# Three PSUM banks for transposed units, one for the products, in a fused attention and two-MLP kernel

## The chip, the cores and the metric

The kernel runs on one core of one Trainium2 chip. The metric is the device time of one execution in microseconds (us); lower is better. TensorE multiplies matrices into PSUM, VectorE, ScalarE and GpSimd do the work on elements, and SyncE issues the transfers (DMA). Each engine runs its own instructions in their order, and waits on counters that the other engines raise.

## What is computed

```python
scores = scale * np.matmul(q, k.transpose(0, 1, 3, 2))      # 2 batches, 12 heads, 448 x 64
scores = np.where(mask, -1000000000.0, scores)              # causal
scores = scores - np.max(scores, axis=-1, keepdims=True)
attn = np.exp(scores)
attn = attn / (np.sum(attn, axis=-1, keepdims=True) + 1e-09)
x = np.matmul(attn, v)                                      # heads side by side: 896 x 768
gate = 1.0 / (1.0 + np.exp(-(x @ w_gate)))
x = gate * (x @ w_val) @ w_out                              # 896 x 1536, then 896 x 768
h = x @ w_in                                                # 896 x 1024
ln = layer_norm(h * softmax(h)) * g_ln
out = ln @ w_out2
```

All of it is fp32. A factor of a matrix product is split into a high part and the rest, its low part, and three products (high with high, high with low, low with high) are added up in PSUM.

## The kernel before

The attention comes first, for twelve pairs of heads (0 to 11). Its order is written out by hand: the table `STEPS` holds for each piece of work a step number, an engine and a function; pair p does the piece with number n at step 8p + n. At every step the loop goes through TensorE ('E'), ScalarE ('A'), VectorE ('D'), SyncE ('S') and GpSimd ('P'), and takes an engine's pieces in the order of the table. So eight steps make one period, in which three pairs are worked on: pair p begins with its scores, pair p - 1 is transposed and multiplied with v, and the product of pair p - 2 is scaled and put away. One period on the engines:

- TensorE. `sc_mm(p)` (L352, L365) writes the masks and the score products into PSUM tiles s. Then, for pair p - 1, `tr_mm` (L435) transposes the exponentials in four units t, numbered 0 to 3 (four 128 x 128 blocks each, one PSUM bank each), and `pv_mm` (L466) multiplies them with v in eight chunks, all into one bank x. A period holds: scores of p; chunk 3; unit 0; chunks 4, 5; unit 1; chunks 6, 7; unit 2; chunks 0, 1; unit 3; chunk 2. Chunks 3 to 7 end the product of p - 2, chunk 0 begins that of p - 1.
- VectorE. `sc_max` (L380) takes row maxima of the scores; `tr_lo` (L231) forms the low part of a transposed unit; `prep_q_lo` (L252) the low part of q; `recips` (L400, L401) the reciprocal row sums; `x_mul` (L472) scales the finished product x into xf.
- ScalarE. `sc_exp` (L392) does the exponentials, `tr_hi` (L442) copies the high part of a unit, `x_hi` (L223) that of the scaled product. In a period: unit 3; `x_hi`; exponential of score tile 3, first head; unit 0; three more exponentials (tile 3, second head; tile 0, both heads); unit 1; tile 2; unit 2; tile 1.
- GpSimd. High parts of q and k (`prep_q_hi` L236, `prep_k_hi` L225), low part of k (`prep_k_lo` L231), both parts of v, the sums and `x_lo`.
- SyncE. `rs_rows` (L406, tile rd) writes the reciprocals to DRAM and `rs_bcast` (L412, tile rb) reads them back, spread over 64 partitions, for `x_mul`; `load_qk` (L214) and `load_v` (L219) fetch later pairs, `dma_next` (L100) the raw MLP weights (768 KB a chunk).

The PSUM pools (L201 to L203) are two banks for units (`ps_t`), two for products (`ps_x`) and four for scores (`ps_s`). A new tile of a pool waits until all that reads the tile which held its bank is done: with two banks, unit 2 waits for the `tr_lo` of unit 0 two units earlier, and a product for the `x_mul` two pairs earlier.

After the attention come gate and value products (L639), the output product (L669), the second MLP's products (L701, L762), with weights that arrive chunk by chunk. The loop that the steps run in, and the pieces that the change touches, are printed here.

Of the kernel before, what the change touches and what calls it, by code (L numbers as in the profile page):

```python
# [43 lines left out]
def attn_moe_moe2(ctx: ExitStack, tc: tile.TileContext, qk, v, w_gv, w_out, w_in2, w_out2, g_ln, out):  # L44
# [149 lines left out]
    with ExitStack() as actx:  # L194
# [3 lines left out]
        ptp = actx.enter_context(tc.tile_pool(name="ptp", bufs=2, side="right"))  # L198
        xfp = actx.enter_context(tc.tile_pool(name="xfp", bufs=2, side="right"))
        drm = actx.enter_context(tc.tile_pool(name="drm", bufs=2, space=bass.MemoryType.DRAM))  # L200
        ps_t = actx.enter_context(tc.tile_pool(name="ps_t", bufs=2, space=PSUM, reuse_waits="tile"))  # L201
        ps_x = actx.enter_context(tc.tile_pool(name="ps_x", bufs=2, space=PSUM, reuse_waits="tile"))
        ps_s = actx.enter_context(tc.tile_pool(name="ps_s", bufs=2, space=PSUM, reuse_waits="tile"))  # L203

        NH = B * H
# [38 lines left out]

        def prep_k_lo(p):
            sub('P' if p else 'D', qk_sp[p][:, 3], qk_raw[p][:, 1], f32(qk_sp[p][:, 0]))
            if p:
                load_qk(p + 2)

        def prep_q_lo(p):  # L250
            t = qk_sp[p]
            nc.vector.scalar_tensor_tensor(out=t[:, 2], in0=qk_raw[p][:, 0], scalar=0.125, in1=f32(t[:, 1]),  # L252
                                           op0=ALU.mult, op1=ALU.subtract)

        def v_parts(p):
            return (v_raw[p % 2][:, 0:3].rearrange("p j (a d) -> p j a d", a=2),
# [60 lines left out]
        def keep_warm(ps, n):  # L317
            for _ in range(n):
                nc.tensor.matmul(out=ps[:, :128], lhsT=idle, rhs=idle, start=True, stop=True)
# [14 lines left out]

        def sc_mask(p, g):
            if p < 2 and g == 0:
                both = [ps_x.tile([128, 512], F32, tag="x", name="s") if p else
                        ps_t.tile([128, 512], F32, tag="t", name="s") for _ in range(2)]
            else:
                pair = ps_s.tile([128, 2, 512], F32, tag="s", name="s")  # L340
                both = [pair[:, a] for a in range(2)]
            c0 = 0
            for i in GROUPS[g]:
                n = QE[i]
                ps = ps_sc[p, i] = [b[:, c0:c0 + n] for b in both]
                if p > 1 or g:
                    ps_both[p, i] = pair[:, :, c0:c0 + n]
                for k in (0, 1) if i else (1,):
                    for e in range(2):
                        rows = slice(e * D, (e + 1) * D)  # L350
                        c = D * (1 - k) if e else n - D * (2 - k)
                        nc.tensor.matmul(out=ps[1 - e][:, c:c + D], lhsT=mk_l[rows, k], rhs=mk_r[rows, k],  # L352
                                         start=(c0 == 0 and k == 0), stop=False, skip_group_check=True)
                c0 += n
# [75 lines left out]
            return 512 if u else S  # L430

        def tr_mm(p, u):
            ps = ps_tr[p, u] = ps_t.tile([128, 512], F32, tag="t", name="t")
            for c, k in tr_blocks(u):
                nc.tensor.transpose(ps[:, max(c, 0):max(c, 0) + 128], p_t[p % 2][:, k:k + 128],  # L435
                                    ident if c >= 0 else identx)
# [7 lines left out]
        def tr_lo(p, u):  # L444
            w = tr_width(u)
            sub('D', pt_t[p][:, 1, u, :w], ps_tr.pop((p, u))[:, :w], f32(pt_t[p][:, 0, u, :w]))
# [39 lines left out]
        def early_tiles():  # L486
# [33 lines left out]
            (14, 'A', lambda p: tr_hi(p, 2)), (6, 'A', lambda p: sc_exp(p, (1,)), 1),  # L520
            (-1, 'D', lambda p: sc_max(p, 3, 0), 2, 3),
            (0, 'D', lambda p: sc_max(p, 3, 0), 3), (16, 'D', lambda p: tr_lo(p, 3)),
            (-7, 'D', prep_q_lo, 3), (9, 'D', recips),
            (2, 'D', lambda p: sc_max(p, 2), 2), (11, 'D', lambda p: tr_lo(p, 0), 1), (3, 'D', lambda p: sc_max(p, 1), 2),
            (13, 'D', lambda p: tr_lo(p, 1)), (21, 'D', x_mul), (15, 'D', lambda p: tr_lo(p, 2)),
            (8, 'P', sums, 1), (9, 'P', prep_v_lo, 1), (25, 'P', x_lo, 0, NPR - 1), (23, 'P', x_lo, NPR - 1),
            (9, 'S', rs_rows), (9, 'S', rs_bcast),
            (-10, 'P', prep_k_hi, 3), (-9, 'P', prep_q_hi, 3), (-4, 'P', prep_k_lo, 3), (7, 'P', prep_v_hi, 1),
        )

# [15 lines left out]
        for e in range(2):  # L546
            sc_max_of(1, e, 3, 0)
        sc_exp(1, (3, 0), (0,))
        keep_warm(ps_t.tile([128, 512], F32, tag="t", name="warm"), 26)
        tr_mm(0, 0)  # L550
        tr_mm(0, 1)
        prep_q_lo(2)
# [20 lines left out]
        for s in range(PER * NPR + 26):  # L573
            steps(s, 'E')
            for _ in range(2):
                if s >= PER * NPR and left and next(early):
                    left -= 1
            steps(s, 'A')
            steps(s, 'D')
            steps(s, 'S')  # L580
            steps(s, 'P')
            if s in (8, 12):
                dma_next()

            for c in range(2 * NE + 2):
                e = s - 88 - 8 * c
                if e in (3, 5, 7):
                    next(bits_now)
                if e == 8 and c < 2 * NE:
                    chunk_hi(c)  # L590
                if e == 9 and c < 2 * NE:
                    chunk_lo(c)
                if e == 0:
                    bits_now = bits_steps(c)
                    next(bits_now)
# [237 lines left out]
```

## Time and profile before

| | us |
|---|---|
| median of 3 runs | 497.45 (496.03 to 497.69) |
| the profiled execution | 497.59 |
| its span, first to last instruction | 495.8 |
| attention: scores of pair 3 begin / of pair 11 begin | 23.16 / 88.98 |
| busy: TensorE / VectorE / ScalarE / GpSimd | 481.9 / 329.7 / 221.8 / 120.8 |

The profiled execution took 1.8 us more than its span. Times in a timeline count from the start of the span. "Busy" is time with an instruction under way. A timeline row may stand for several equal instructions (x8); what stands in brackets is how long the engine was idle before it and what ended that. PE is TensorE, DVE VectorE, ACT ScalarE, POOL GpSimd, SPq SyncE's queue.

### The profile page before, as it was taken

The page shows a single profiled execution, that of the slowest core. Times are in us where ns is not written, and L with a number is a line of the kernel's source. Part 1 is how long each engine was busy: PE and PEld are TensorE (multiplying, and loading weights), DVE is VectorE, ACT ScalarE, POOL GpSimd, SP SyncE. Part 2 cuts the span into 40 slices and gives each one's busy share as a digit, 9 for nine tenths or more (in the row PEclk, how much of TensorE's full clock was granted, in tenths as well). Part 3 has the DMA queues.
Part 4 walks back from the last instruction along what each step waited for, and adds up shares of the span by engine and source line. Part 5 has one row for each costly group of instructions (what it writes and reads, how often), then busy time and mean ns, then how long its engine had stood idle before and what let it go on. Part 6 is the DMA issues. An engine that isn't in the chain of part 4 may idle for free.

```text
span 495.8 us, 7596 instructions
## 1 busy us (share of the span) xinstructions
PE 481.9 (97%) x2907; PEld 440.8 (89%) x2907; DVE 329.7 (67%) x508; ACT 221.8 (45%) x471; POOL 120.8 (24%) x190
## 2 busy tenths in 40 slices
PE   8979988999999999999999999999999999999997
PEld 7868878899999999999999999999988888899996
DVE  7788888887556788777779647777635887821110
ACT  6868787955334434534543423433421433323111
POOL 5749878530000000000000000000060778610000
PEclk9999999999999999999999999999999999999999
DMA  5454433243322535433444333533431221001001
GB/s 192 138 156 148 155 93 104 61 147 127 129 76 94 169 131 167 153 117 116 167 159 139 127 108 127 167 128 116 163 128 26 103 69 60 0 33 62 34 32 65
DMA packets 15685, 55.60 MB, mean 112 GB/s; under 512 B 2720, under 2 KB 4768, under 8 KB 15648
## 3 DMA queue, kind: packets, MB, share of 16 engines
q1 hardware_dynamic: 15648, 55.11, 33.1%
q8 instruction: 23, 0.38, 0.3%
q14 instruction: 14, 0.11, 0.1%
HBM read 52.30 MB, written 2.80 MB: 111 GB/s over the span
## 4 chain that ended last, share of the span: by engine, by line
PE 84%; DVE 7%; DMA 4%; issue 2%; ACT 1%; SPq 1%; DVEq 0%; ACTq 0%
PE gv L639 34%; PE pm L669 18%; PE po L762 12%; PE h L701 12%; DVE pt L231 2%; PE x L466 2%; DVE sum L380 2%; PE t L435 2%; PE gv L498 2%; DVE qks L252 2%; PE s L365 1%; DMA rd<-rs32q 1%; DMA rb<-rd 1%; PE tp L744 1%; DMA qkr<-in_qk_dram 1%
## 5 line engine op out<-in xcount | busy, mean ns | idle before, releaser
L639 PE MATMUL gv<-xy,hl 128*128 128x448 f32 x828 | 168.1, 365 | 0.0
L639 PEld LDWEIGHTS gv<-xy,hl 128*128 128x128 f32 x828 | 155.4, 188 | 12.3
L669 PE MATMUL pm<-g,hl 128*128 128x448 f32 x432 | 87.7, 365 | 0.0
L669 PEld LDWEIGHTS pm<-g,hl 128*128 128x128 f32 x432 | 81.1, 188 | 6.4
L686 POOL TENSOR_SCALAR t<-t,g_sb 128x768 f32<-128x768 f32 x8 | 9.0, 1124 | 247.7 <-PE pm L669 247.7
L134 DVE TENSOR_TENSOR hl<-t,hl 128x768 fp32r<-128x768 f32 x36 | 35.1, 975 | 40.8 <-ACT hl L131 39.1
L762 PE MATMUL po<-wo,lt 128*128 128x384 f32 x336 | 60.7, 340 | 0.0
L701 PE MATMUL h<-wi,xy 128*128 128x512 f32 x252 | 59.3, 396 | 0.0
L762 PEld LDWEIGHTS po<-wo,lt 128*128 128x128 f32 x336 | 58.7, 188 | 0.2 <-POOL wo L691 0.2
L701 PEld LDWEIGHTS h<-wi,xy 128*128 128x128 f32 x252 | 47.1, 187 | 11.4
L117 DVE SCALAR_TENSOR_TENSOR t<-raw,t 128x768 int32<-128x768 int32 (+1 forms) x56 | 52.6, 939 | 1.8
L120 DVE SCALAR_TENSOR_TENSOR t<-raw,t 128x768 int32<-128x768 int32 (+1 forms) x56 | 52.0, 929 | 1.7
L112 ACT ACTIVATE raw<-raw 128x768 f32<-128x768 f32 (+1 forms) x56 | 48.2, 867 | 9.2 <-DMA raw<-in_wo_dram 5.9
L466 PE MATMUL x<-pt,v 128*128 128x384 f32 (+3 forms) x252 | 51.0, 324 | 0.0
L392 ACT ACTIVATE p<-s,sum 128x320 f32<-128x320 f32 (+3 forms) x92 | 43.7, 494 | 14.4 <-DVE sum L380 11.1
L466 PEld LDWEIGHTS x<-pt,v 128*128 128x128 f32 x252 | 37.0, 190 | 1.6
L231 DVE TENSOR_TENSOR pt<-t,pt 128x512 fp32r<-128x512 f32 (+1 forms) x48 | 32.0, 666 | 4.7 <-ACT pt L442 4.6
L171 DVE TENSOR_TENSOR lt<-tp,lt 128x512 fp32r<-128x512 f32 x14 | 9.7, 690 | 36.4 <-ACT lt L170 36.4
L435 PE MATMUL t<-ident,p 128*128 128x128 f32 x180 | 28.0, 276 | 5.6 <-DVE pt L231 5.6
L115 DVE TENSOR_SCALAR t<-raw 128x768 int32<-128x768 int32 (+1 forms) x56 | 30.6, 546 | 2.7 <-ACT raw L112 2.7
L380 DVE TENSOR_REDUCE sum<-s 128x2 f32<-128x640 f32 (+3 forms) x44 | 28.8, 677 | 5.1 <-PE s L365 5.1
L131 ACT CAST hl<-t 128x768 fp32r<-128x768 f32 x36 | 30.0, 834 | 4.6 <-PE pm L669 4.2
(97 smaller groups left out, 481.6 us busy)
## 6 DMA issues: line engine op xcount, KB each, us to landing
raw<-in_gv_dram SPq DMA_DIRECT2D x24, 768.0 KB
raw<-in_wo_dram SPq DMA_DIRECT2D x20, 768.0 KB
raw<-in_wi_dram SPq DMA_DIRECT2D x12, 512.0 KB
qkr<-in_qk_dram SPq DMA_DIRECT2D x11, 448.0 KB
vr<-in_v_dram SPq DMA_DIRECT2D x12, 256.0 KB
rb<-rd SPq DMA_DIRECT2D x24, 112.0 KB
out_dram<-o SPq DMA_DIRECT2D x6, 384.0 KB
rd<-rs32q SPq DMA_DIRECT2D x48, 1.0 KB
```

What stands on the lines that cost most here:

```text
L112: nc.scalar.activation(out=w1.bitcast(F32), in_=w1.bitcast(F32), func=AF.Copy, scale=2.0 ** -112)
L117: nc.vector.scalar_tensor_tensor(out=tt, in0=w1, scalar=-2 ** 31, in1=tt, op0=ALU.bitwise_and, op1=ALU.bitwise_or)
L120: nc.vector.scalar_tensor_tensor(out=tt, in0=w0, scalar=29, in1=tt, op0=ALU.logical_shift_right, op1=ALU.bitwise_or)
L231: (nc.gpsimd if eng == 'P' else nc.vector).tensor_tensor(out=out, in0=a, in1=b, op=ALU.subtract)
L380: nc.vector.reduce_max(out=sum_t[p % 3][:, 8 + 2 * i:10 + 2 * i], in_=ps_both[p, i], axis=AX.X, negate=True)
L392: nc.scalar.activation(out=p_t[p % 2][:, POFF[i] + (1 - e) * n:POFF[i] + (2 - e) * n], in_=ps_sc[p, i][1 - e], func=AF.Exp, bias=mx, scale ...
L435: nc.tensor.transpose(ps[:, max(c, 0):max(c, 0) + 128], p_t[p % 2][:, k:k + 128], ident if c >= 0 else identx)
L466: nc.tensor.matmul(out=ps[:, q0:], lhsT=l, rhs=pt_t[pr][:, c, u, c0:c0 + S - q0], start=(chunk == 0 and n == 0), stop=(chunk == 7 and n == ...
L639: nc.tensor.matmul(out=ps[i, b], lhsT=w[:, a, cs], rhs=xy[kk][:, x, b * S:(b + 1) * S], start=(kk == 0 and a == 0 and x == 0), stop=(kk == ...
L669: nc.tensor.matmul(out=ps[b], lhsT=w[:, a, cs], rhs=g_t[kk][:, x, b * S:(b + 1) * S], start=(kk == 0 and a == 0 and x == 0), stop=(kk == N ...
L701: nc.tensor.matmul(out=h[:, n * 512:(n + 1) * 512], lhsT=xy[kk][:, a, tk], rhs=wi[n * NK + kk][:, c], start=(kk == 0 and i == 0), stop=(kk ...
L762: nc.tensor.matmul(out=ps[n], lhsT=lts[k // 4][:, a, k % 4], rhs=wo[k][:, c, cs], start=(k == 0 and i == 0), stop=(k == NF2 - 1 and i == 2))
```

## The change

The pool of units gets three banks and the pool of products one. The score tiles of pairs 0 and 1 that borrowed from these pools are dealt out anew, and the warm-up matmuls write into the bank that unit 0 of pair 0 then takes. `prep_q_lo` moves from step -7 to step -2, behind `x_mul` of the same period, and takes the load of q and k for two pairs later with it (for pairs above 2). The reciprocals and their two transfers move from step 9 to step 10. The first two raw weight loads move from steps 8 and 12 (pair 1) to steps 44 and 52 (pairs 5 and 6).

```diff
@@ -198,8 +198,8 @@
         ptp = actx.enter_context(tc.tile_pool(name="ptp", bufs=2, side="right"))
         xfp = actx.enter_context(tc.tile_pool(name="xfp", bufs=2, side="right"))
         drm = actx.enter_context(tc.tile_pool(name="drm", bufs=2, space=bass.MemoryType.DRAM))
-        ps_t = actx.enter_context(tc.tile_pool(name="ps_t", bufs=2, space=PSUM, reuse_waits="tile"))
-        ps_x = actx.enter_context(tc.tile_pool(name="ps_x", bufs=2, space=PSUM, reuse_waits="tile"))
+        ps_t = actx.enter_context(tc.tile_pool(name="ps_t", bufs=3, space=PSUM, reuse_waits="tile"))
+        ps_x = actx.enter_context(tc.tile_pool(name="ps_x", bufs=1, space=PSUM, reuse_waits="tile"))
         ps_s = actx.enter_context(tc.tile_pool(name="ps_s", bufs=2, space=PSUM, reuse_waits="tile"))
 
         NH = B * H
@@ -244,13 +244,15 @@
 
         def prep_k_lo(p):
             sub('P' if p else 'D', qk_sp[p][:, 3], qk_raw[p][:, 1], f32(qk_sp[p][:, 0]))
-            if p:
+            if 0 < p < 3:
                 load_qk(p + 2)
 
         def prep_q_lo(p):
             t = qk_sp[p]
             nc.vector.scalar_tensor_tensor(out=t[:, 2], in0=qk_raw[p][:, 0], scalar=0.125, in1=f32(t[:, 1]),
                                            op0=ALU.mult, op1=ALU.subtract)
+            if p > 2:
+                load_qk(p + 2)
 
         def v_parts(p):
             return (v_raw[p % 2][:, 0:3].rearrange("p j (a d) -> p j a d", a=2),
@@ -334,8 +336,8 @@
 
         def sc_mask(p, g):
             if p < 2 and g == 0:
-                both = [ps_x.tile([128, 512], F32, tag="x", name="s") if p else
-                        ps_t.tile([128, 512], F32, tag="t", name="s") for _ in range(2)]
+                both = [ps_x.tile([128, 512], F32, tag="x", name="s") if p > e else
+                        ps_t.tile([128, 512], F32, tag="t", name="s") for e in range(2)]
             else:
                 pair = ps_s.tile([128, 2, 512], F32, tag="s", name="s")
                 both = [pair[:, a] for a in range(2)]
@@ -430,7 +432,9 @@
             return 512 if u else S
 
         def tr_mm(p, u):
-            ps = ps_tr[p, u] = ps_t.tile([128, 512], F32, tag="t", name="t")
+            if (p, u) not in ps_tr:
+                ps_tr[p, u] = ps_t.tile([128, 512], F32, tag="t", name="t")
+            ps = ps_tr[p, u]
             for c, k in tr_blocks(u):
                 nc.tensor.transpose(ps[:, max(c, 0):max(c, 0) + 128], p_t[p % 2][:, k:k + 128],
                                     ident if c >= 0 else identx)
@@ -520,11 +524,11 @@
             (14, 'A', lambda p: tr_hi(p, 2)), (6, 'A', lambda p: sc_exp(p, (1,)), 1),
             (-1, 'D', lambda p: sc_max(p, 3, 0), 2, 3),
             (0, 'D', lambda p: sc_max(p, 3, 0), 3), (16, 'D', lambda p: tr_lo(p, 3)),
-            (-7, 'D', prep_q_lo, 3), (9, 'D', recips),
+            (10, 'D', recips),
             (2, 'D', lambda p: sc_max(p, 2), 2), (11, 'D', lambda p: tr_lo(p, 0), 1), (3, 'D', lambda p: sc_max(p, 1), 2),
-            (13, 'D', lambda p: tr_lo(p, 1)), (21, 'D', x_mul), (15, 'D', lambda p: tr_lo(p, 2)),
+            (13, 'D', lambda p: tr_lo(p, 1)), (21, 'D', x_mul), (-2, 'D', prep_q_lo, 3), (15, 'D', lambda p: tr_lo(p, 2)),
             (8, 'P', sums, 1), (9, 'P', prep_v_lo, 1), (25, 'P', x_lo, 0, NPR - 1), (23, 'P', x_lo, NPR - 1),
-            (9, 'S', rs_rows), (9, 'S', rs_bcast),
+            (10, 'S', rs_rows), (10, 'S', rs_bcast),
             (-10, 'P', prep_k_hi, 3), (-9, 'P', prep_q_hi, 3), (-4, 'P', prep_k_lo, 3), (7, 'P', prep_v_hi, 1),
         )
 
@@ -546,7 +550,8 @@
         for e in range(2):
             sc_max_of(1, e, 3, 0)
         sc_exp(1, (3, 0), (0,))
-        keep_warm(ps_t.tile([128, 512], F32, tag="t", name="warm"), 26)
+        ps_tr[0, 0] = ps_t.tile([128, 512], F32, tag="t", name="t")
+        keep_warm(ps_tr[0, 0], 26)
         tr_mm(0, 0)
         tr_mm(0, 1)
         prep_q_lo(2)
@@ -579,7 +584,7 @@
             steps(s, 'D')
             steps(s, 'S')
             steps(s, 'P')
-            if s in (8, 12):
+            if s in (44, 52):
                 dma_next()
 
             for c in range(2 * NE + 2):
```

Where this moves instructions, by the order in which they stand on an engine (names: s scores, t transposed unit, pt its two parts, x product, xf the scaled product; a counter such as DVE_49 is the one that VectorE raises, Activation_49 ScalarE's, PE_49 TensorE's own). Lines of the changed kernel are up to five higher.

VectorE, one period from the first maxima on; before, and then with the change:

```order
L380 TENSOR_REDUCE sum_146<-s 128x2 x2
L231 TENSOR_TENSOR pt<-t,pt 128x512
L252 SCALAR_TENSOR_TENSOR qks<-qkr,qks 128x448
L400 RECIPROCAL rs32t_152<-rs8i_150 128x8
L401 STREAM_TRANSPOSE rs32q_154<-rs32t_152 128x32
L380 TENSOR_REDUCE sum_146<-s 128x2
L231 TENSOR_TENSOR pt<-t,pt 128x448
L380 TENSOR_REDUCE sum_146<-s 128x2
L231 TENSOR_TENSOR pt<-t,pt 128x512
L472 TENSOR_TENSOR xf<-x,rb 128x448
L231 TENSOR_TENSOR pt<-t,pt 128x512
```

```order
L382 TENSOR_REDUCE sum_148<-s 128x2 x2
L231 TENSOR_TENSOR pt<-t,pt 128x512
L402 RECIPROCAL rs32t_151<-rs8i_149 128x8
L403 STREAM_TRANSPOSE rs32q_153<-rs32t_151 128x32
L382 TENSOR_REDUCE sum_148<-s 128x2
L231 TENSOR_TENSOR pt<-t,pt 128x448
L382 TENSOR_REDUCE sum_148<-s 128x2
L231 TENSOR_TENSOR pt<-t,pt 128x512
L476 TENSOR_TENSOR xf<-x,rb 128x448
L252 SCALAR_TENSOR_TENSOR qks<-qkr,qks 128x448
L231 TENSOR_TENSOR pt<-t,pt 128x512
```

The low part of q (the row with qks) stood third, ahead of the reciprocals; it stands now behind xf, the scaling of the product. The scaling itself keeps its place behind the low part of unit 1.

TensorE, from the last chunks of one product over unit 2 to the first chunk of the next, with what each waits for; before, and then with the change:

```order
L466 MATMUL x<-pt,v_0_142 128x256 x2
L466 MATMUL x<-pt,v_0_142 128x128 x3
L466 MATMUL x<-pt,v_0_142 128x256 x3
L435 MATMUL t<-ident,p_158 128x128 [waits DVE_49,PE_49]
L435 MATMUL t<-ident,p_158 128x128 x3
L466 MATMUL x<-pt,v_1_145 128x448 [waits Activation_49,Pool_49]
L466 MATMUL x<-pt,v_1_145 128x448
L466 MATMUL x<-pt,v_1_145 128x448 [waits Pool_49]
L466 MATMUL x<-pt,v_1_143 128x384 [waits Activation_49]
```

```order
L470 MATMUL x<-pt,v_0_142 128x128 x3
L470 MATMUL x<-pt,v_0_142 128x256 x3
L439 MATMUL t<-ident,p_158 128x128 [waits PE_49]
L439 MATMUL t<-ident,p_158 128x128 x3
L470 MATMUL x<-pt,v_1_145 128x448 [waits DVE_49,Activation_49,Pool_49]
L470 MATMUL x<-pt,v_1_145 128x448
L470 MATMUL x<-pt,v_1_145 128x448 [waits Pool_49]
L470 MATMUL x<-pt,v_1_143 128x384 [waits Activation_49]
```

Unit 2 no longer waits for VectorE. The first matmul of the product now does: for the scaling of the product before it, whose bank it takes.

SyncE's queue in pairs 1 and 2, from the load of v on; before, and then with the change:

```order
L219 DMA vr_113<-in_v_dram 128x512
L100 DMA raw<-in_gv_dram 128x1536
L406 DMA rd<-rs32q_153 8x32 x4
L412 DMA rb<-rd 64x448 x2
L100 DMA raw<-in_gv_dram 128x1536
L406 DMA rd<-rs32q_154 8x32 x4
L412 DMA rb<-rd 64x448 x2
L219 DMA vr_114<-in_v_dram 128x512
```

```order
L219 DMA vr_113<-in_v_dram 128x512
L408 DMA rd<-rs32q_153 8x32 x4
L414 DMA rb<-rd 64x448 x2
L219 DMA vr_114<-in_v_dram 128x512
L408 DMA rd<-rs32q_154 8x32 x4
L414 DMA rb<-rd 64x448 x2
L214 DMA qkr<-in_qk_dram 128x896
```

The two raw weight loads that stood around the first reciprocals (rd, rb) are gone from here, and stand in pairs 5 and 6.

## Rows read from the trace of the kernel before

**Rows 1.** Busy time by stretch: us, then busy (instructions) by engine, clock, DMA share.

```profile
60.00:75.00 15.00, 13.69 (x146) 12.44 (x144) 12.58 (x23) 12.29 (x42) 11.34 (x17) 1.00 0.37 119
...
90.00:105.00 15.00, 13.86 (x111) 12.65 (x110) 14.69 (x25) 11.30 (x31) 7.98 (x10) 1.00 0.29 94
...
200.00:300.00 100.00, 100.00 (x495) 92.66 (x494) 72.60 (x101) 42.38 (x65) 0.00 (x0) 1.00 0.40 135
```

**Rows 2.** Waits of TensorE, whole span: total us, times, longest us.

```profile
PE t L435 <- DVE pt L231: 8.3, 12, 1.5
```

**Rows 3.** Timeline of TensorE, one pair of heads: start us, length us, instruction.

```profile
57.21 0.26 PE L352 MATMUL s<-mk_r,mk_l 64*128 64x64 bf16 x6
...
61.17 1.17 PE L466 MATMUL x<-pt,v 128*128 128x256 f32 x8
...
63.00 0.66 PE L435 MATMUL t<-ident,p 128*128 128x128 f32 x4 [0.66 <-DVE pt L231]
...
63.41 1.03 PE L466 MATMUL x<-pt,v 128*128 128x448 f32 x4
...
65.16 0.26 PE L352 MATMUL s<-mk_r,mk_l 64*128 64x64 bf16 x6
```

**Rows 4.** Timeline of VectorE, the same pair.

```profile
58.45 1.29 DVE L380 TENSOR_REDUCE sum<-s 128x2 f32<-128x896 f32 x2 [0.64 <-PE s L365]
...
60.26 1.08 DVE L252 SCALAR_TENSOR_TENSOR qks<-qkr,qks 128x448 fp32r<-128x448 f32 x1
...
61.27 0.19 DVE L400 RECIPROCAL rs32t<-rs8i 128x8 f32<-128x8 f32 x1
...
62.33 0.62 DVE L231 TENSOR_TENSOR pt<-t,pt 128x448 fp32r<-128x448 f32 x1
...
63.32 0.68 DVE L231 TENSOR_TENSOR pt<-t,pt 128x512 fp32r<-128x512 f32 x1
...
63.92 0.62 DVE L472 TENSOR_TENSOR xf<-x,rb 128x448 f32<-128x448 f32 x1
...
65.08 0.69 DVE L231 TENSOR_TENSOR pt<-t,pt 128x512 fp32r<-128x512 f32 x1 [0.54 <-ACT pt L442]
```

**Rows 5.** Timeline of ScalarE, the same pair.

```profile
59.86 0.64 ACT L392 ACTIVATE p<-s,sum 128x448 f32<-128x448 f32 x1 [1.01 <-DVE sum L380]
...
62.10 0.61 ACT L442 CAST pt<-t 128x512 fp32r<-128x512 f32 x1
...
64.46 0.58 ACT L442 CAST pt<-t 128x512 fp32r<-128x512 f32 x1
```

**Rows 6.** Timeline of TensorE in the last pair, where no wait stands at 93.95.

```profile
92.94 1.18 PE L466 MATMUL x<-pt,v 128*128 128x256 f32 x8
93.95 0.60 PE L435 MATMUL t<-ident,p 128*128 128x128 f32 x4
94.31 1.03 PE L466 MATMUL x<-pt,v 128*128 128x448 f32 x4
...
97.28 0.33 PE L435 MATMUL t<-identx,p 128*128 128x128 f32 x1 [0.71 <-DVE pt L231]
```

**Rows 7.** Timeline of TensorE: the masks that begin pair 3 and pair 11.

```profile
23.16 0.26 PE L352 MATMUL s<-mk_r,mk_l 64*128 64x64 bf16 x6
...
88.98 0.26 PE L352 MATMUL s<-mk_r,mk_l 64*128 64x64 bf16 x6
```

**Rows 8.** Timeline of VectorE: products of pairs 0 and 9 and what stands ahead.

```profile
21.12 0.68 DVE L231 TENSOR_TENSOR pt<-t,pt 128x512 fp32r<-128x512 f32 x1
25.97 0.62 DVE L472 TENSOR_TENSOR xf<-x,rb 128x448 f32<-128x448 f32 x1 [4.17 <-DMA rb<-rd]
...
95.15 0.61 DVE L472 TENSOR_TENSOR xf<-x,rb 128x448 f32<-128x448 f32 x1
```

**Rows 9.** Timeline of SyncE's queue: the first raw weight load.

```profile
14.17 0.42 SPq L100 DMA_DIRECT2D raw<-in_gv_dram  x1
```

**Rows 10.** Busy time by stretch: the last figures are DMA share and GB/s.

```profile
16.00:18.00 2.00, 1.50 (x13) 1.33 (x11) 1.61 (x4) 2.00 (x9) 0.77 (x3) 1.00 0.96 296
```

## The prediction

> **What bounds the kernel now.** I read the busy time by stretch first [rows 1]. After the attention TensorE is busy for 100.00 of 100 us, so all that the attention loses or gains should reach the end one for one. In the attention TensorE is busy for 13.69 of 15 us, so time is lost there, and none of the other engines is full (VectorE 12.58, ScalarE 12.29). TensorE's waits [rows 2] name one cause for nearly all of it: transposes that wait for VectorE's low parts, 8.3 us in 12 waits. So I took one period of the timeline, the one that begins with the scores of pair 7, and looked for the ring of waits that sets its length. The period runs from masks to masks, 57.21 to 65.16, so 7.95 us [rows 3]. In it TensorE reaches unit 2 and waits 0.66 us for the low part of unit 0.
>
> The ring closes like this. From the masks to the first row maximum, 57.21 to 58.45, it is 1.24 us [rows 3, 4]. VectorE then works from 58.45 to the low part of unit 0 at 62.33 without a pause: 3.88 us, of which q's low part takes 1.01 (60.26 to 61.27) [rows 4]. That low part takes 0.62 and its hand-off to the transposes of unit 2, at 63.00, another 0.05. From there to the next masks at 65.16 it is 2.16 us [rows 3]. The sum is 1.24 + 3.88 + 0.67 + 2.16 = 7.95 us, the whole period: VectorE's queue with q's low part in it sets the pace, and the two banks of units hand that on to TensorE.
>
> What TensorE would need without a wait comes from the last pair, which has no next q to prepare [rows 6]: chunks 6 and 7 to unit 2 take 1.01 us (92.94 to 93.95) and unit 2 to chunk 0 0.36 us. In the shown period the first of these is 1.83 us (61.17 to 63.00), the second 0.41. Without the wait a period would last 7.95 - 0.82 - 0.05 = 7.08 us.
>
> **The change, part by part.** *Third bank of units.* Unit 2 no longer waits for the low part of unit 0. That removes 0.87 us a period, if nothing else is late. *q's low part* leaves the ring. At its new place, behind the scaling, VectorE has the pause before 65.08, 0.54 us, and the one before the next maxima, 0.64 us [rows 4], so I cost it at nothing; with that cover gone it would cost its 1.01 us again. Its load of q and k goes with it and is issued behind VectorE's scaling instead of behind GpSimd's low part of k; it now stands ahead of the load of v in SyncE's queue, and is used a period later. I cost that at nothing too. *Reciprocals a step later:* they lead to the scaling of the next period, some 11 steps off; nothing.
>
> *One bank for products* is what I think decides. Chunk 0 of a product must now wait until the scaling of the product before it has been read out of the bank. Behind chunk 0 all of TensorE's queue waits: unit 3, chunk 2 and the next scores, and through these the next maxima and exponentials. When is the scaling done? It stands on VectorE behind the low part of unit 1, which needs ScalarE's high part of unit 1, and that stands in ScalarE's queue behind four exponentials of the new pair, which need the new maxima. So there is a second ring. From masks to maxima it is 1.24 us as before. From the maxima to the first exponential (58.45 to 59.86) it is 1.41, from there to the high part of unit 1 (62.10) 2.24, without a gap [rows 4, 5]. From the start of a high part to a low part that waits for it, I read 0.62 at unit 2 (64.46 to 65.08); unit 1's copy is 0.03 longer, so 0.65. From that low part to the scaling it is 0.60 (63.32 to 63.92). The scaling takes 0.62 and its hand-off, which no row shows, the 0.05 of the other hand-off: 0.67. That is 6.81 us from masks to chunk 0. From chunk 0 to the next masks it is 1.75 (63.41 to 65.16) [rows 3]. The ring is 8.56 us long.
>
> VectorE without q's low part would reach the low part of unit 1 at 1.24 + (63.32 - 58.45) - 1.01 = 5.10 us after the masks; ScalarE lets it start at 1.24 + 1.41 + 2.24 + 0.65 = 5.54. So ScalarE's queue sets the ring, and freeing VectorE can't shorten it. TensorE, without waits, would reach chunk 0 at 6.81 - 1.48 = 5.33 us; it stands 1.48 us there, where before it stood 0.87 at unit 2. **Each period gets 8.56 - 7.95 = 0.61 us longer.** I allow 0.1 us either way for hand-offs.
>
> From the masks of pair 3 to those of pair 11 there are eight periods, 23.16 to 88.98, so 65.82 us [rows 7]. Eight times 8.56 is 68.48: **+2.7 us** (8.46 gives +1.9, 8.66 gives +3.5). This counts what the early pairs lose now: they stand in the 65.82.
>
> *The early pairs and the raw loads.* The first scaling now stands at 25.97, 4.17 us late for its broadcast reciprocals [rows 8], which sit in the queue behind a raw load of 768 KB issued at 14.17 [rows 9]. The change takes that load away. At 296 GB/s [rows 10] it is 2.6 us of transfer, so the scaling comes at 23.4 us or sooner, and no sooner than the low part ahead of it lets it: 21.12 + 0.60 = 21.72. No row tells where between; I take the middle, 22.5. Until now this lateness was hidden from chunk 0 of pair 1; with one bank it is not. Chunk 0 then starts at 22.5 + 0.67 and pair 3 begins 1.75 later, at 24.9 instead of 23.16: **+1.8 us** (from 24.14, +1.0, to 25.8, +2.7). In pairs 5 and 6 the raw loads stand behind the reciprocals of that period and ahead of a load that is used a period later; I cost them at nothing, and at 2.6 us if they delay GpSimd.
>
> *The last pairs.* There VectorE is busy 14.69 of 15 us with weight preparation as well [rows 1]. Chunk 0 of pair 10 started at 94.31; now it follows the scaling at 95.15 [rows 8], so at 95.8, 1.5 us late. Behind it TensorE had waited 0.71 us for VectorE at 97.28 [rows 6], a wait that the third bank removes. About half is left: **+0.7 us** (0 to 1.5).
>
> The sum is 2.7 + 1.8 + 0.7 = +5.2 us on the profiled execution's 497.59, which is 0.14 above the median of 497.45: **502.7 us**. The bounds add up to +2.9 and +7.7, so 500.4 to 505.2.
>
> The first half of the change removes the wait that the profile names; the second half puts a longer one in its place. The Trainium skill speaks against that half: its page "Perfetto Trace Analysis", section "Matmuls", says that independent groups of matmuls should rotate through different PSUM banks, so that the evacuation of one overlaps the matmuls of the next. By that rule alone, which prices only the evacuation, the result would be the first rival's 494; the rows say that the evacuation's place in the queues costs more than its length.
>
> **The rivals.** *Faster: the scaling is not held up by the queue.* If it started as soon as its product was done, at 0.05 us after 62.34 (61.17 + 1.17) in the shown period [rows 3], it would free the bank 0.67 later, 5.85 us after the masks. That is 0.52 later than TensorE comes, the period would be 7.60, and eight of them 60.8, so -5.0; with +1.0 and +0.3 at the ends the time would be some 494. With the +1.8 and +0.7 above the sign turns at a ring of 7.9 us, that is, if the high part of unit 1 were ready some 0.65 us sooner. The order of both queues speaks against it. I give it 5%. *No change:* the early pairs gain the most and the ring is 8.1 us, half a microsecond shorter than my sum; eight of them, 64.8, and +1.0 at the start cancel: about 497.6. 6%. *Worse:* the raw loads in pairs 5 and 6 make a scaling or GpSimd late, twice 2.6 us on top: 507.9. 4%. The counters that the first product matmul waits for include VectorE's, so the wait is surely there; a case where the change does nothing is not needed.
>
> **How the numbers follow.** My forecast has 85%, the rivals 5, 6 and 4. The range that should hold 8 in 10 is 499.5 to 505.0: the forecast's bounds, a little lower toward the second rival. About 0.3%, 1.5 us, is what a measurement can tell from no change. Slower by more than that: 0.85 + 0.04 = 0.89; faster: 0.06 (the first rival and a little of the second); within: 0.05.
>
> **What would show it.** In the changed profile transposes should wait for VectorE's low parts hardly at all, and chunk 0 (x behind unit 2) should wait about 1.5 us a period for the scaling xf, with a period of 8.5 to 8.6 us. VectorE should wait for ScalarE's high part of unit 1. Pair 3 should begin near 25 and pair 11 near 93.4. If the period is below 7.95, or the wait at chunk 0 under 0.9 us, the second ring is wrong; if the wait is there but ends with a transfer, the reciprocals are late, not ScalarE.

## The result, and the profile after

The changed kernel takes **502.82 us** (median of 4 runs, 502.57 to 503.01), the one before, run beside it, 497.57. The ratio is 1.0106, 95% interval 1.0076 to 1.0136: slower by 1%, 0.1 us from the forecast. The profiled execution took 502.57 us with a span of 500.8. Of all executions below one stands outside its ratio, the first profiled one of run 8 at 952.16 us. Lines have moved: transposes are L439, products L470, the scaling L476, high parts of units L446.

Busy time by stretch, after, to be held against [rows 1] (us, then busy time and instructions by engine, clock, DMA share, GB/s):

```profile
60.00:75.00 15.00, 12.35 (x118) 11.31 (x117) 12.54 (x24) 11.28 (x40) 9.81 (x15) 1.00 0.45 153
200.00:300.00 100.00, 100.00 (x495) 92.70 (x494) 73.32 (x102) 40.47 (x62) 0.00 (x0) 1.00 0.41 140
```

Behind the attention TensorE is full as before, so the loss lies in the attention alone: TensorE is busy there for 12.35 of 15 us where it was 13.69. No other engine took up the time. VectorE does the same 12.5 us; the new loss is waiting.

TensorE's waits from 8 to 130 us, after (total us, times, longest us):

```profile
PE x L470 <- DVE xf L476: 13.4, 11, 1.4
```

The row of [rows 2], transposes that wait for VectorE's low parts, is gone. Products that wait for the scaling took its place, with 13.4 us against 8.3: 5.1 us more, and the time is 5.25 us longer.

Now one period, to be held against [rows 3, 4, 5]. TensorE's timeline, after (start us, length us, instruction, idle time before it and what ended that):

```profile
58.66 0.26 PE L354 MATMUL s<-mk_r,mk_l 64*128 64x64 bf16 x6
...
63.62 0.60 PE L439 MATMUL t<-ident,p 128*128 128x128 f32 x4
65.54 1.03 PE L470 MATMUL x<-pt,v 128*128 128x448 f32 x4 [1.33 <-DVE xf L476]
...
67.29 0.26 PE L354 MATMUL s<-mk_r,mk_l 64*128 64x64 bf16 x6
```

VectorE's timeline, same stretch:

```profile
59.89 1.29 DVE L382 TENSOR_REDUCE sum<-s 128x2 f32<-128x896 f32 x2 [1.90 <-PE s L367]
...
64.17 0.69 DVE L231 TENSOR_TENSOR pt<-t,pt 128x512 fp32r<-128x512 f32 x1 [0.34 <-ACT pt L446]
64.78 0.62 DVE L476 TENSOR_TENSOR xf<-x,rb 128x448 f32<-128x448 f32 x1
65.31 0.89 DVE L252 SCALAR_TENSOR_TENSOR qks<-qkr,qks 128x448 fp32r<-128x448 f32 x1
66.12 0.68 DVE L231 TENSOR_TENSOR pt<-t,pt 128x512 fp32r<-128x512 f32 x1
```

ScalarE's timeline, same stretch:

```profile
61.30 0.63 ACT L394 ACTIVATE p<-s,sum 128x448 f32<-128x448 f32 x1 [1.84 <-DVE sum L382]
...
63.53 0.61 ACT L446 CAST pt<-t 128x512 fp32r<-128x512 f32 x1
...
65.01 0.63 ACT L446 CAST pt<-t 128x512 fp32r<-128x512 f32 x1
```

The ring can be walked row by row. Masks to maxima 1.23 us (58.66 to 59.89), to the first exponential 1.41 (61.30), to the copy of unit 1 2.23 (63.53), to its low part 0.64 (64.17, which ends an idle 0.34 and names the copy), to the scaling 0.61 (64.78), to chunk 0 0.76 (65.54), to the next masks 1.75 (67.29). The sum is the period, 8.63 us. Unit 2, at 63.62, follows chunks 6 and 7 without a wait; chunk 0 behind it waits 1.33. VectorE itself now idles 1.90 us ahead of the maxima.

TensorE, after: pair 3, pair 11 and the last two waits, to be held against [rows 6, 7]:

```profile
24.12 0.26 PE L354 MATMUL s<-mk_r,mk_l 64*128 64x64 bf16 x6
...
93.17 0.26 PE L354 MATMUL s<-mk_r,mk_l 64*128 64x64 bf16 x6
...
100.09 1.03 PE L470 MATMUL x<-pt,v 128*128 128x448 f32 x4 [1.36 <-DVE xf L476]
...
102.03 0.29 PE L439 MATMUL t<-identx,p 128*128 128x128 f32 x1
...
107.09 0.65 PE L470 MATMUL x<-pt,v 128*128 128x448 f32 x2 [0.36 <-DVE xf L476]
```

The 5 us come in three pieces. Pair 3 begins 0.96 us later (24.12 against 23.16). The eight periods to pair 11 take 69.05 us against 65.82, so 3.23 more. The last pairs lose another 0.8: the spans differ by 5.0, and 4.19 are there at pair 11.

VectorE's first scaling, after, to be held against [rows 8]:

```profile
20.78 0.68 DVE L231 TENSOR_TENSOR pt<-t,pt 128x512 fp32r<-128x512 f32 x1
21.60 0.62 DVE L476 TENSOR_TENSOR xf<-x,rb 128x448 f32<-128x448 f32 x1
```

No wait for a transfer is listed for it any more; it stood at 25.97 with a wait of 4.17. It begins 0.82 us behind the low part ahead of it, where 0.60 is usual [rows 4]; what the other 0.22 are, no view shows.

### The profile page after: what moved, and what is told of

Same layout as the page of the kernel before. It is cut to its first block, busy times and chain, and to the rows that moved or that the text cites. A ratio compares the mean times of both kernels' runs of the same rounds, so it can differ in the third digit from the quotient of the medians.

```text
span 500.8 us, 7576 instructions
## 1 busy us (share of the span) xinstructions
PE 481.9 (96%) x2907; PEld 440.6 (88%) x2907; DVE 326.4 (65%) x508; ACT 221.9 (44%) x471; POOL 118.5 (24%) x190
## 4 chain that ended last, share of the span: by engine, by line
PE 83%; ACT 5%; issue 4%; DVE 3%; DMA 2%; POOL 2%; SPq 0%; DVEq 0%; ACTq 0%; POOLq 0%
PE gv L644 34%; PE pm L674 17%; PE po L767 12%; PE h L706 12%; ACT p L394 3%; PE x L470 3%; ACT pt L446 2%; PE s L367 2%; PE gv L502 1%; DMA qkr<-in_qk_dram 1%; PE tp L749 1%; DVE xf L476 1%; PE t L439 1%; DVE sum L382 1%; DVE pt L231 1%
## 5 line engine op out<-in xcount | busy, mean ns | idle before, releaser
L470 PE MATMUL x<-pt,v 128*128 128x384 f32 (+3 forms) x252 | 51.0, 324 | 13.4 <-DVE xf L476 13.4
L470 PEld LDWEIGHTS x<-pt,v 128*128 128x128 f32 x252 | 37.0, 190 | 17.5 <-POOL v L225 12.1
L446 ACT CAST pt<-t 128x512 fp32r<-128x512 f32 (+1 forms) x48 | 28.3, 590 | 9.6 <-PE t L439 9.6
```

The costliest lines, as they stand in the source:

```text
L446: nc.scalar.copy(out=pt_t[p][:, 0, u, :w], in_=ps_tr[p, u][:, :w])
L470: nc.tensor.matmul(out=ps[:, q0:], lhsT=l, rhs=pt_t[pr][:, c, u, c0:c0 + S - q0], start=(chunk == 0 and n == 0), stop=(chunk == 7 and n == ...
```

## The experiments

My theory: with one product bank, chunk 0 waits for the scaling, and the scaling is late because it stands behind the low part of unit 1 on VectorE, which waits for a copy behind four exponentials on ScalarE. Rivals: the bank does it whatever the order of the queues; VectorE's own load does it; the moved transfers do it. Each run changes one thing. The kernel before was run beside each of them, with medians of 496.5 to 497.6 us, so a difference of about 1 us between two runs says little.

**1. The scaling ahead of the low part of unit 1**, in the changed kernel:

```diff
-            (13, 'D', lambda p: tr_lo(p, 1)), (21, 'D', x_mul), (-2, 'D', prep_q_lo, 3), ...
+            (21, 'D', x_mul), (13, 'D', lambda p: tr_lo(p, 1)), (-2, 'D', prep_q_lo, 3), ...
```

> The changed kernel, with the scaling of the product placed ahead of the low part of unit 1 in VectorE's order. Theory (the bank is held by the scaling's place behind ScalarE's copy of unit 1): the scaling starts when its product is done, 5.2 us after the masks, chunk 0 0.76 later at 5.9, so a period of 7.7 us instead of 8.63, eight of them 7.5 us less, about 495 us in all. Rival (one bank costs this much wherever the scaling stands, by the evacuation and its hand-offs): the wait at chunk 0 stays near 1.3 us, 502 to 503 us.

Measured: 494.54 us, ratio to the kernel before 0.9948 (0.9928 to 0.9969). TensorE:

```profile
60.83 1.03 PE L470 MATMUL x<-pt,v 128*128 128x448 f32 x4 [0.37 <-DVE xf L476]
...
68.52 1.03 PE L470 MATMUL x<-pt,v 128*128 128x448 f32 x4 [0.37 <-DVE xf L476]
```

One swap of two neighbours on VectorE gives back 8.3 us and turns the change into a gain, with one product bank as before. The period is 7.69 us (60.83 to 68.52) and the wait at chunk 0 0.37. So most of the time is not the price of one bank as such, but of the place of its evacuation in VectorE's queue; what one bank costs even so, run 3 tells. For the changed kernel's weight loads at chunk 0 the list of waits mostly names GpSimd's v (12.1 us in 8 waits). GpSimd's queue is untouched here, and the wait falls even so, so it was not what set it.

**2. The copy of unit 1 ahead of the two exponentials of tile 0** on ScalarE, in the changed kernel:

```diff
-            ... (2, 'A', lambda p: sc_exp(p, (0,)), 2),
-            (12, 'A', lambda p: tr_hi(p, 1), 1), ...
+            ... (11, 'A', lambda p: tr_hi(p, 1), 1),
+            (3, 'A', lambda p: sc_exp(p, (0,)), 2), ...
```

> The changed kernel, with ScalarE's copy of unit 1 ahead of the two exponentials of score tile 0. Theory (second ring through ScalarE's queue): the copy comes 0.6 us sooner; then VectorE's own queue, which reaches the low part of unit 1 at 5.1 us after the masks, takes over from ScalarE at 5.5, so the period falls by 0.4 to 8.2 us, and the time to 499 or 500 us. Rival (the product's evacuation sets the wait): nothing changes, 502.8 us.

Measured: 499.29 us, ratio 1.0043 (1.0026 to 1.0061). TensorE:

```profile
57.06 0.26 PE L354 MATMUL s<-mk_r,mk_l 64*128 64x64 bf16 x6
...
63.52 1.03 PE L470 MATMUL x<-pt,v 128*128 128x448 f32 x4 [0.90 <-DVE xf L476]
...
65.27 0.26 PE L354 MATMUL s<-mk_r,mk_l 64*128 64x64 bf16 x6
```

The period is 8.21 us, 0.42 shorter, and the wait 0.43 shorter. VectorE's queue is untouched here, so it is ScalarE's queue that held the ring, as the theory says.

**3. Two banks each again**, with q's low part, the reciprocals and the raw loads in their new places (the score tiles and the warm-up are dealt out as before again):

```diff
-ps_t = ... bufs=3 ...
-ps_x = ... bufs=1 ...
+ps_t = ... bufs=2 ...
+ps_x = ... bufs=2 ...
```

> The changed kernel with two banks for units and two for products again; q's low part, the reciprocals and the raw loads stay where the change put them. Theory: unit 2's wait for VectorE is gone already because q's low part left the ring (the low part of unit 0 ends 4.8 us after the masks, TensorE reaches unit 2 at 5.0); no wait at chunk 0; unit 3 waits under 0.1 us for the low part of unit 1. Period 7.1 to 7.2 us, about 491 us in all. Rival (the third bank is what removes the wait at unit 2): that wait comes back, the period is 7.9 and the time 496 to 498 us.

Measured: 490.74 us, ratio 0.987 (0.9849 to 0.9891), the best of all so far. TensorE:

```profile
53.20 0.26 PE L354 MATMUL s<-mk_r,mk_l 64*128 64x64 bf16 x6
...
60.40 0.26 PE L354 MATMUL s<-mk_r,mk_l 64*128 64x64 bf16 x6
...
66.35 0.66 PE L437 MATMUL t<-ident,p 128*128 128x128 f32 x4 [0.82 <-DVE pt L231]
...
68.52 0.26 PE L354 MATMUL s<-mk_r,mk_l 64*128 64x64 bf16 x6
```

The period is 7.20 to 7.25 us, and unit 2 waits in none but one of the periods (60.40 to 68.52, 8.12 us), though only two unit banks are there. So unit 2 did not need the third bank: moving q's low part had removed its wait already. Nor are the moved transfers the cause of the loss; they are all still in their new places here. The split of the banks costs 12.1 us of the changed kernel's time.

**4. The banks alone**, in the kernel before (the edit of 3 the other way, with the score tiles and warm-up dealt out as in the change):

```diff
-ps_t = ... bufs=2 ...
-ps_x = ... bufs=2 ...
+ps_t = ... bufs=3 ...
+ps_x = ... bufs=1 ...
```

> The kernel before, with three banks for units and one for products and nothing else moved. Theory: with q's low part still in VectorE's queue the low part of unit 1 starts 6.1 us after the masks, chunk 0 1.37 later, so a period of 9.2 us; with the late first scaling 5 to 6 us on top at the start: 511 to 513 us. Rival (the loss comes from moving q's low part or the loads, not from the banks): 503 us or less.

Measured: 510.91 us, ratio 1.029 (1.026 to 1.0321). VectorE, and TensorE's chunk 0:

```profile
65.40 1.29 DVE L380 TENSOR_REDUCE sum<-s 128x2 f32<-128x896 f32 x2 [1.90 <-PE s L365]
...
67.20 0.93 DVE L252 SCALAR_TENSOR_TENSOR qks<-qkr,qks 128x448 fp32r<-128x448 f32 x1
...
70.11 0.68 DVE L231 TENSOR_TENSOR pt<-t,pt 128x512 fp32r<-128x512 f32 x1
70.70 0.61 DVE L474 TENSOR_TENSOR xf<-x,rb 128x448 f32<-128x448 f32 x1
...
71.46 1.03 PE L468 MATMUL x<-pt,v 128*128 128x448 f32 x4 [1.75 <-ACT p L392]
```

From the maxima to the low part of unit 1 it is 4.71 us, without idle time on VectorE, against 4.28 in the changed kernel (59.89 to 64.17), where ScalarE set it. With q's low part in the queue VectorE is the later of the two, and the period is 9.05 us (the list names ScalarE's exponentials for the wait at chunk 0, but from the scaling to chunk 0 it is 0.76 as in the changed kernel). So this part of the change alone costs 14 us. Not all of it is waiting: in the profiled execution TensorE's clock fell twice (last section), at 25.04, where chunk 0 to the masks took 3.21 us instead of 1.75, and in the period from 82.25 to 92.65, 10.40 us instead of 9.05. By an estimate from these rows that is 2.8 us.

**5. q's low part alone**, with its load, in the kernel before:

```diff
-            if p:
+            if 0 < p < 3:
                 load_qk(p + 2)
...
+            if p > 2:
+                load_qk(p + 2)
...
-            (-7, 'D', prep_q_lo, 3), (9, 'D', recips),
+            (9, 'D', recips),
...
-... (21, 'D', x_mul), (15, 'D', lambda p: tr_lo(p, 2)),
+... (21, 'D', x_mul), (-2, 'D', prep_q_lo, 3), (15, 'D', lambda p: tr_lo(p, 2)),
```

> The kernel before, with q's low part (and its load) moved behind the product's scaling and nothing else. Theory: the move by itself takes the wait at unit 2 out, two banks suffice; a period of 7.1 to 7.2 us from pair 4 on instead of 7.95, seven of them 5 to 6 us, while the early loss from the raw loads stays: about 492 us. Rival (the move needs the third bank): 497 us.

Measured: 494.04 us (7 runs, 490.77 to 494.85), ratio 0.9935 (0.991 to 0.996). TensorE:

```profile
32.72 0.26 PE L354 MATMUL s<-mk_r,mk_l 64*128 64x64 bf16 x6
...
39.92 0.26 PE L354 MATMUL s<-mk_r,mk_l 64*128 64x64 bf16 x6
```

The period is 7.20 us with this move alone, as expected; the time is 2 us above the expected 492. The profiled execution took 491.74, the median is 2.3 us longer. The spread goes with TensorE's clock: the two executions below 492 us have a mean granted clock of 0.999 and 1.000, the five from 494.04 to 494.85 one of 0.993 to 0.997. What made the clock fall in them can't be read from the one profiled execution and stays open.

**6. The raw loads alone**, in the kernel before:

```diff
-            if s in (8, 12):
+            if s in (44, 52):
```

> The kernel before, with the two raw loads moved to pairs 5 and 6 and nothing else. Theory: the first scaling comes near 21.7 us instead of 26, so the period of pair 3 falls from 10.65 to about 8 us and the later ones stay at 7.95: 494 to 495 us. Rival (the loads only shift the loss into pairs 5 and 6): 497 us.

Measured: 494.69 us, ratio 0.9958 (0.9945 to 0.9971). TensorE's masks of pair 4, and VectorE's first scaling:

```profile
30.87 0.26 PE L352 MATMUL s<-mk_r,mk_l 64*128 64x64 bf16 x6
...
21.61 0.61 DVE L472 TENSOR_TENSOR xf<-x,rb 128x448 f32<-128x448 f32 x1
```

The period stays near 7.93 us. The gain is at the start: pair 4 begins at 30.87 where it began at 33.81, and the spans differ by 3.0 us, the medians by 2.1.

**7. The raw loads back at steps 8 and 12**, in the changed kernel:

```diff
-            if s in (44, 52):
+            if s in (8, 12):
```

> The changed kernel, with the first two raw weight loads issued in pair 1 again. Theory: the first scaling is late for its reciprocals as before, near 26 us instead of 21.6, and with one bank that goes straight into chunk 0 of pair 1: 4 us more, 506 to 507 us. Rival (the raw loads moved nothing that counts): 502.8 us.

Measured: 507.01 us (504.79 to 508.23), ratio 1.0191 (1.0157 to 1.0224). TensorE, and VectorE's first scaling:

```profile
24.43 1.26 PE L470 MATMUL x<-pt,v 128*128 128x448 f32 x4 [3.17 <-DVE xf L476]
...
27.12 0.34 PE L354 MATMUL s<-mk_r,mk_l 64*128 64x64 bf16 x6
...
23.66 0.62 DVE L476 TENSOR_TENSOR xf<-x,rb 128x448 f32<-128x448 f32 x1 [2.24 <-DMA rb<-rd]
```

The loads are worth 4.2 us in the changed kernel (507.01 to 502.82) and 2.1 in the one before (run 6). With one bank the late first scaling stops TensorE at chunk 0, as the prediction has it. But it came at 23.66, not near 26 as the expectation has it, and the time was met for another reason. In the profiled execution, whose span is 3.6 us longer than the changed kernel's, 2.06 us are the scaling (23.66 against 21.60) and 1.55 TensorE's clock after the wait (last section). The one execution with a mean granted clock of 1.000 took 504.79, only 2.0 us more than the changed kernel.

**8. The raw loads behind q's rows, in pairs 5 and 7.** In run 3 the long period began when GpSimd waited 3.43 us for q's rows, which SyncE issued just behind a raw load. So I put the loads at steps 47 and 63, behind those rows, in run 3's kernel:

```diff
-            if s in (44, 52):
+            if s in (47, 63):
```

> The kernel with two and two banks again (q's low part, reciprocals as in the change), with the raw loads one at step 47 and one at 63, behind the load of q and k of their pair instead of ahead of it. Theory: the one long period (8.12 us, the scores of pair 7 on), in which GpSimd waited 3.43 us for q and k behind a raw load, falls to 7.2: 0.9 us less, about 489.8 us. Rival (the reciprocals behind the raw load then come late instead): no gain, 490.7 us.

Measured: 489.63 us (489.34 to 489.72, and the one of 952.16), ratio 0.9852 (0.9834 to 0.987). Then once more, for a profile:

> The same kernel as the run with two and two banks and the first raw loads in pairs 5 and 7, behind q's transposed rows, for a profile of it. Theory: 489.6 us; all periods from pair 3 to pair 11 are 7.21 us, no period of 8.1 us with a wait of GpSimd for q's rows as in the run with the raw loads ahead of them. Rival: the long period is there with the raw loads behind the rows too, and the gain over that run (490.74) is chance.

Measured: 490.98 us, ratio 0.9886 (0.985 to 0.9921). The two results of one kernel bracket run 3's 490.74, so the move is worth nothing that can be measured, and the long period is still there (59.11 to 67.55, 8.44 us). SyncE's queue of this run says why:

```profile
47.32 0.43 SPq L100 DMA_DIRECT2D raw<-in_gv_dram  x1
...
48.28 1.37 SPq L408 DMA_DIRECT2D rd<-rs32q  x4
54.52 1.21 SPq L414 DMA_DIRECT2D rb<-rd  x2
55.85 0.52 SPq L214 DMA_DIRECT2D qkr<-in_qk_dram  x1
```

Its waits from 36 to 66 us:

```profile
SPq L414 <- DMA rd<-rs32q: 11.2, 4, 4.3
```

The reciprocals (rd, 1 KB a piece) were issued behind the 768 KB raw load, landed late, and SyncE stood up to 4.3 us in front of the read-back (rb) that waits for them. The next rows of q (qkr) are queued behind that read-back and were issued at 55.85, 9.1 us after the ones before. GpSimd waited 3.53 us for them. My reading of run 3 was at best half of it: the raw load a period earlier delays q's rows too, through rd and rb. In run 3 SyncE stood 3.1 us in front of the read-back ahead of the late rows, and 4.6 us in front of the next. The load just ahead has a share as well: in run 3 those rows were issued at 56.44 and GpSimd began with them at 62.42, 6.0 us later; without a load just ahead it is 4.7 here (55.85 to 60.54). A run that puts the loads behind rb's wait was not made.

**9. The copy of unit 1 early and two banks each**: the edit of run 2, in the kernel of run 8.

```diff
-            ... (2, 'A', lambda p: sc_exp(p, (0,)), 2),
-            (12, 'A', lambda p: tr_hi(p, 1), 1), ...
+            ... (11, 'A', lambda p: tr_hi(p, 1), 1),
+            (3, 'A', lambda p: sc_exp(p, (0,)), 2), ...
```

> Two banks for transposed units and two for products, q's low part and the reciprocals in their new places, the first raw loads in pairs 5 and 7 behind q's transposed rows, and the copy of unit 1 ahead of the exponential of tile 0 on ScalarE. My theory: with two product banks TensorE waits for nothing at unit 2 and chunk 0 in a steady period (7.21 us, TensorE's own work), so an earlier copy has no wait to take away: 489.3 to 489.9 us, the same as with the copy in its place. Rival: the copy still sets the period in some place that the trace does not show as a wait, and the time falls by 1 us or more (488.5 or less).

Measured: 490.2 us (488.32 to 490.63), ratio 0.985 (0.9821 to 0.988). TensorE:

```profile
51.38 0.26 PE L354 MATMUL s<-mk_r,mk_l 64*128 64x64 bf16 x6
58.46 0.26 PE L354 MATMUL s<-mk_r,mk_l 64*128 64x64 bf16 x6
```

The weight load (PEld) of unit 3 in run 3:

```profile
52.25 0.42 PEld L437 LDWEIGHTS t<-ident,p 128*128 128x128 f32 x4 [0.26 <-DVE pt L231]
```

The expectation took 7.21 us for TensorE's own work; that was wrong. The period is 7.08 us, the value that the prediction had worked out from the last pair. In 7.21 there is still 0.13 of waiting, at unit 3: with two banks it waits for the low part of unit 1, and its weight load stood 0.26 to 0.28 us for that in the steady periods of run 3, in none of those here. The matmuls' own list of waits does not show it. Eight times 0.13 is 1 us, but the periods behind the raw loads are longer here (58.46 to 66.15, 7.69 us, and 73.24 to 81.99, 8.75), and from pair 3 to pair 11 only 0.4 us is left (58.90 against 59.31 in run 8). The median lies between the two of run 8: a gain in the time is not shown. The versions with two banks each, at 490 to 491 us, beat both kernels.

## Why the prediction was right

*The bound and the second ring.* Right in place and cause, and near in size. Runs 1 and 2 move the two queue places that the ring names, and each takes away what the ring says. Six of its seven terms hold to 0.01 us; the seventh, the hand-off from the scaling to chunk 0, was borrowed from another pair of instructions as 0.05 and measures 0.14 (0.76 from start to start, less the 0.62 of the scaling). That makes a ring of 8.63 us where 8.56 was forecast, and over eight periods +3.2 where it was +2.7. The list of waits gives 1.33 us at chunk 0, less than the forecast's 1.48, because it counts from the end of unit 2; chunk 0 stands 6.88 us after the masks, 1.55 later than the 5.33 that TensorE would need.

*The early pairs* were mis-sized: +0.96, not +1.8. The step that failed is the middle that I took for the first scaling, 22.5 between 21.72 and 23.4. It came at 21.60, on the early end, and no wait for a transfer is listed there. What was wrong was to take off no more than the load's transfer, 2.6 us: run 6, which moves the loads alone, has the scaling at 21.61, so the load had cost all of the 4.17 us of waiting. SyncE's queue before shows how: the reciprocals (rd) were issued behind the load, and SyncE stood 5.1 us in front of their read-back (before, 8 to 24 us):

```profile
SPq L412 <- DMA rd<-rs32q: 5.1, 1, 5.1
```

In the changed order the load would cost 2.06 (23.66 in run 7, with 2.24 us of waiting for rb).

*The last pairs:* +0.8 against +0.7, in part by luck. Counted from the masks of pair 11, chunk 0 of pair 10 comes 1.59 us later than before (6.92 against 5.33), as forecast (1.5). But at the transposes that had waited 0.71 us no more than 0.56 of it is left (8.86, at 102.03, against 8.30), and a second wait for a scaling, 0.36 us at 107.09, which the working does not have, is part of the 0.8. The three sizes sum to +5.0 for +5.2; an error of +0.5 and one of -0.8 cancel in part, so the time is nearer than its terms.

*q's low part at nothing:* right. But the cover was not the pause that the prediction names. The low part of unit 2 begins behind q's low part at 66.12 and waits for no copy (which began at 65.01), where it had waited 0.54 us; in this period q's low part takes 0.89 us and holds it up by some 0.5. That costs nothing because the ring does not run through it: the period from 41.39 to 50.02, where q's low part takes 0.62, is 8.63 us as well. Run 5 shows that this move by itself takes the wait at unit 2 away, and here the prediction missed something: it gave the removal of the first ring to the third bank, and said only that freeing VectorE can't shorten the second. Run 3 shows that with q's low part gone two banks of units are enough for unit 2. The third bank bought next to nothing that the other move had not: the 0.13 us a period at unit 3 (run 9).

*The raw loads in pairs 5 and 6 at nothing:* right for this kernel, but for a reason the prediction lacked. They do delay rows of q. GpSimd waits 2.29 us for them at 64.16 in the changed kernel, and its period there is 8.63 us all the same; at 7.21 us (run 3) the same loads cost one period 0.9. I take the wait at chunk 0 for the slack that hides them. So the mechanism of the rival that made it worse exists, and the slow ring covered it.

*The rule.* By the faster rival the time was 494, if the bank were freed as soon as its product is done; run 1 brings this about in VectorE's queue and measures 494.54. The Trainium skill, "Perfetto Trace Analysis", section "Matmuls", asks to rotate independent groups through different PSUM banks; run 3 and the changed kernel, 490.74 and 502.82, agree with its direction. The price is not one number: 12.1 us with the evacuation behind another engine's queue, 3.8 (run 1 to run 3) with it moved ahead.

## What to carry to other kernels

Before a buffer is taken from one pool and given to another, follow the evacuation that frees the last one back through every queue that it stands in: its own length (0.62 us here) says little, its place in the queues (1.33 us of waiting a period) is the price, and moving one instruction ahead of its neighbour gave back 8.3 of the 12.1 us here. Of two edits that remove the same wait, try each alone; here the move of one VectorE instruction made the third bank all but pointless. And a delay that is costed at nothing because something waits longer elsewhere comes back when that is mended.

## What the runs showed of the hardware

**TensorE's clock after a long wait.** In run 7 chunk 0 waited 3.17 us. Busy time by stretch of that run (the figure behind the engines is the granted clock):

```profile
24.00:26.00 2.00, 1.57 (x7) 1.43 (x8) 1.83 (x3) 0.00 (x0) 1.55 (x2) 0.76 0.90 357
26.00:28.00 2.00, 2.00 (x15) 1.52 (x15) 0.00 (x0) 1.05 (x2) 0.29 (x1) 0.50 0.06 22
```

After the wait the granted clock fell to 0.50, which is 1.2 GHz of 2.4, and was back at 1.00 from 30 us on. The four matmuls of chunk 0 took 1.26 us, against 1.03 in the changed kernel, and from chunk 0 to the masks it is 2.69 us where the changed kernel needs 1.75. So 0.94 us is lost to the clock there, on top of the wait, and 0.6 more at the next scores (27.12 to 28.76 is 1.64 us, in the changed kernel 1.04). Run 4's wait of 3.87 us in the same place was followed by the same fall, to 0.70 and 0.50. Waits of 1.33 us a period left the clock at 1.00 in the changed kernel. In run 4 chunk 0 waits 1.4 to 1.75 us in each later period, and there the clock stayed at 1.00 behind all of these waits up to 80.50 (the one at 71.46 is shown in run 4), but fell behind the one at 89.55:

```profile
89.55 1.68 PE L468 MATMUL x<-pt,v 128*128 128x448 f32 x4 [1.73 <-ACT p L392]
...
90.00:92.00 2.00, 2.00 (x9) 1.83 (x8) 0.63 (x1) 0.72 (x4) 1.12 (x2) 0.50 0.43 161
```

So waits of nearly one length were followed by different clocks; what set the last apart, these rows do not show.

**VectorE and GpSimd in each other's way.** I had taken 1.01 us as what q's low part costs VectorE [rows 4]. Its own length is 0.62, as at 22.14 and 82.56 in the changed kernel. What GpSimd did at the time, before:

```profile
59.70 1.16 POOL L231 TENSOR_TENSOR xy<-xf,xy 128x448 fp32r<-128x448 f32 x1
60.80 1.55 POOL L231 TENSOR_TENSOR qks<-qkr,qks 128x448 fp32r<-128x448 f32 x1
```

And after:

```profile
65.22 1.14 POOL L225 TENSOR_SCALAR v<-vr 128x384 fp32r<-128x384 f32 x2
...
72.37 0.77 POOL L225 TENSOR_SCALAR v<-vr 128x384 fp32r<-128x384 f32 x2 [0.46 <-PE x L470]
```

Before, q's low part starts at 60.26, while GpSimd's instruction of 59.70 runs until about 60.80, and lasts 0.46 us longer than alone. GpSimd's next one, from 60.80, lasts 1.55 where others like it take 1.14. After, it overlaps two GpSimd instructions from 65.22: VectorE's takes 0.27 more, GpSimd's pair 1.14 where it takes 0.77 undisturbed. By these rows each waits while the other has its turn, and no longer. The Trainium skill says so too ("SBUF — State Buffer", section "Who interferes with whom"): a VectorE instruction with two SBUF inputs and a GpSimd instruction that reads SBUF exclude each other, and the later one blocks. The rows agree: from 60.26 to 60.80 would be a wait of 0.54, and 0.46 is lost. So, by this reading, 0.46 of the 1.01 us that left the first ring were GpSimd's doing; at the new place six of nine last 0.61 to 0.62.
